# A stored order for five engines, replaced by another: packed attention followed by a gated MLP

## The chip, the cores and the metric

The kernel runs on 1 core of one Trainium2 chip. The metric is device time in microseconds (us) of one execution; lower is better. The kernel before takes 729.8 us (median of 3 runs, 729.75 to 729.95).

## What is computed

There are 8 batches of 8 heads, 576 positions, head size 64, and 32 "packed" queries per head. All inputs of the attention are float32. The MLP weights arrive as float64, eight bytes a value, and are reduced on the chip.

```
p_packed = softmax(p k^T / 8) v          # 32 packed rows per head
out      = softmax(q p_packed^T / 8) p_packed
x  = out, heads side by side             # 4608 tokens x 512
xn = x / rms(x) * rms_g
g  = xn w_gate ;  val = xn w_val         # 512 x 1536 each
y  = (silu(g) * val) w_out               # 1536 x 512
```

## The kernel before

The work is a set of some 270 chains. Each chain is a Python generator that yields a request (an engine and a modelled cost) before each small group of instructions that it emits. The names in `CHAINS` are these: `keys` loads p and k of a batch and transposes k; `stage1 b` computes the packed rows of batch b; `w 0` to `w 11` load one 1 MB float64 piece of w_gate or w_val, turn it into float32 in three passes (L585 on ACT; L588 to L592 on ACT, POOL or DVE; L599 on DVE) and, on each odd piece, find a scale per column group c (L647 to L672); `query u` and `attention u` treat unit u, which is 384 tokens; `pw b` multiplies the packed rows of batch b into the six column groups of the weights (matmuls L1299, after a scaling of a small tile at L1280 or L1282); `pw_evict b c` splits each product into two float16 halves (L548 on ACT, L550 on DVE); `mlp` runs unit after unit: twelve pairs of products of six matmuls (L1706), then three output tiles of 36 matmuls (L1733); `gated u f` evicts a pair (L1742, L1745) and splits it (L1757, L1760); `wo i` and `wo_split i` prepare w_out; `scales` makes the scales of unit 0; `store u i` evicts an output tile and stores it.

Which chain goes next is not decided by a rule at run time. The tuple `ORDER` (L43) has 2805 numbers, each the index of a chain in `CHAINS`. `Plan.run` (L301) walks through it and lets the named chain emit its next group. So `ORDER` fixes the order of the instructions within each of the five queues: PE, ACT, DVE, POOL, and SP, from which all loads and stores are issued. Each queue works in that order, and instructions of different queues are held together by semaphores only.

Two more things come from tables. `BY` (L346) says which engine does a step that several could do; there is one letter per instance (A for ACT, D for DVE, P for POOL), read by `way`. And `Plan.fill` (L279) puts filler matmuls (L1814, products of zeros that nobody reads) into the gaps which the plan's own clock expects on PE in the first stage; that clock uses the modelled costs and `FETCHES` (L58), a list of modelled delays of PE's instruction blocks. The `FETCHES` list reaches the program in no other way.

The first stage lasts until units 0 and 1 have their attention. Its chain for unit 0, by the lines that the rows name, is: scores (L1505, PE), row maxima and differences (L1526, DVE), exponentials (L1531, ACT), row sums and division (L1534 on, DVE), transposes (L1370, PE), copies of these (L1381 on ACT, L1384 on DVE), products with the packed rows (L1583, PE), sums of squares (L1602, ACT), the norm (L1619 on DVE, a power on POOL, L1635 on DVE), scaling (L1656 on ACT, a third of it on DVE), transposes (L1370), and the two float16 halves of the result (L1390 on ACT, L1392 on DVE). Then the first product of `mlp` can run.

Of the kernel before, what the change touches and what calls it, by code (L numbers as in the profile page):

```python
# [45 lines left out]
IN_TURN = range(18)  # L46

FILL = (0.5, 1.0, 400.0, 0.4, 2.5)

TABLE = 1.31  # L50

LOADING = (2.0, 385e3, 0.5)
TURNING = 2.2
COLD = 1.85
WINDOW, KEEP, HEAT = 3.4133, 0.39, 0.73
SWITCH = 0.093
FETCH = 4.3
FETCHES = (8.0, 8.0, 8.0, 8.0, 8.0, 8.0, 5.7397, 7.0078, 4.3, 4.3, 5.5211, 9.0647, 10.3428, 7.075, 6.652, 7.3144, 10.3813, 10.0522, 6.7016, 6.426, 4.3, 6.3087, 7.9214, 8.95, 4.8913, 7.311, 4.3, 4.3, 4.4226, 5.8673, 4.3, 4.3, 6.665, 7.2578, 5.85, 4.3, 7.0863, 14.3121, 6.5442, 9.189, 4.3, 4.3, 8.8812, 5.3336, 6.3223, 4.3, 4.3, 4.3, 6.1668, 7.5087, 4.8472, 4.3, 6.5501, 6.745, 4.3, 4.3, 4.3, 4.9924, 4.3, 4.3, 5.948, 4.3, 4.3)  # L58
FETCH_AT, FETCH_NEED, FETCH_SIZE = 128, 449, 256


def pe(n, count):

    return count * max(n / 2400 + 0.0025, 0.029)

ACT_COST = (0.093, 0.87e-3)
DVE_COST = (0.074, 0.953e-3)

# [13 lines left out]
def way(table, n, steps):  # L84
    by = BY[table][n]
    return by, steps[by]
# [15 lines left out]
class Plan:  # L102
# [160 lines left out]
    def fetched(self, t, cost, n):  # L263
# [4 lines left out]
        for k in range(max(0, (a - FETCH_NEED) // FETCH_SIZE), b // FETCH_SIZE + 1):  # L268
            for at in (FETCH_SIZE * k + FETCH_AT, FETCH_SIZE * (k - 1) + FETCH_NEED):
# [3 lines left out]
                if at == FETCH_SIZE * k + FETCH_AT:  # L273
                    self.avail[k] = x + (FETCHES[k] if k < len(FETCHES) else FETCH)
                else:
# [25 lines left out]
    def run(self, matmul):  # L301
        for n in ORDER:
            self.settle()
            chain = self.named[CHAINS[n]]
            assert isinstance(chain.ask, tuple) and chain.ask[0] in ENGINE, (chain.name, chain.key, chain.ask)
            e = ENGINE[chain.ask[0]]
            t = self.start(chain)
            kind, cost, *_ = chain.ask
            if e == "pe":
                self.fill(t, matmul)  # L310
                t = max(t, self.free["pe"])
            if kind == LOAD:
                self.free[e] = t + 0.45
                self.landed = max(self.landed, t + LOADING[0]) + cost / LOADING[1]
                seen = self.landed + LOADING[2]
            elif kind == TPOSE:
                issue = 0.1 + cost / 786432 * 3.5
                self.free[e] = t + issue
                self.landed = max(self.landed + 0.9 * issue, t + issue)
                seen = self.landed + TURNING  # L320
            else:
                if kind in (EXP, SILU) and kind != self.table:
                    self.table = kind
                if kind == DVE2 or (kind == POOL and len(chain.ask) < 4):
                    cost = self.port(kind, t, cost)
                if e == "pe":
                    cost = self.clocked(t, cost, 1.0 if len(chain.ask) < 4 else chain.ask[3])
                    cost = self.fetched(t, cost, 1 if len(chain.ask) < 5 else chain.ask[4])
                    self.tiled = kind == PET
                self.free[e] = t + cost  # L330
                seen = t + cost + LATENCY[kind]
            chain.end, chain.sent = seen, self.free[e]
            chain.since, chain.engine = 0.0, e
            self.go(chain)
        self.settle()
        assert not self.chains, [(c.key, c.ask) for c in self.chains]
# [6 lines left out]

LATER = {'attention': -1433.963, 'conv': 801.89, 'g': -1062.925, 'gated': 139.94, 'keys': 1179.512, 'mlp': 190.43, 'pw': -303.845, 'pw_evict': -510.85, 'query': 670.065, 'scales': -1237.656, 'stage1': 1107.652, 'store': -164.269, 'v': 1831.937, 'w': 752.946, 'wo': -103.455, 'wo_split': 661.626}

BY = {'low': 'PPAAPAAPAPAP', 'low_wo': 'PPPPPP', 'pgv': 'PPPAPDPPAAAPDAPAAP', 'norm_wo': 'DAAADA', 'keys': 'DADDADAAADAA', 'query': 'ADAAAA', 'hi0': 'DAADDAADDAAA', 'hi1': 'DDDAAAAAAAAA', 'hi_mixed': 'AAAAAAAAAAAA', 'hi_one': 'AAAAAAAAAAAA', 'lo0': 'DPPPDDDPDDPP', 'lo1': 'DPDDPDPDPDDD', 'lo_mixed': 'DPDPPDPDPDDD', 'lo_one': 'PDPDPPPPPDDD', 'gv': 'DPPPDP', 'wo_hi': 'AAPAAD', 'a1t': 'ADAAAA', 'a1t_late': 'AAAAAAAAAAAAAAAAAAAAAAAA', 'scaled': 'DAADDA', 'store': 'DDADDDDDDDDDDDDDDDDDDDDDDDDDDDDDDDDD'}  # L346

RAW_AT = (0, 1, 2, 3, 4, 5, 6, 7, 8, 4, 5, 6)
WO_AT = (8, 3, 7, 8, 3, 8)
# [1546 lines left out]
```

## Time and profile before

| | before |
|---|---|
| median of 3 runs | 729.8 us |
| the profiled execution | 729.18 us |
| its span, first to last instruction | 727.4 us |
| PE busy in the span | 708.4 us (97%) |
| DVE, ACT, POOL busy | 463.8, 454.9, 149.6 us |
| mean granted TensorE clock | 0.999 |

The table is read with one thing in mind: PE is busy for 97% of the span, but that counts the filler matmuls too, and all of its larger gaps lie in the first tenth of the span.

### The profile page before, as it was taken

To read this page: it belongs to the slowest core of one execution; us is meant where nothing else is said; L and a number is where in the kernel's file an instruction comes from. 1 tells how busy PE (TensorE), PEld (TensorE's weight loads), DVE (VectorE), ACT (ScalarE), POOL (GpSimd) and SP (SyncE) were. 2 spreads that over 40 slices of the span, in tenths; PEclk is the share of its full clock that TensorE was granted. 3 is DMA by queue.
4 is the path that set the end of the run, shared out by engine and by line. 5 is a ranking of instruction groups with operands and counts; after the bars stand their busy time and mean duration, and the time that the engine had idled before them with its cause. 6 is when DMAs were issued, how large, how long until landed. Compare 5 with 4: busy or idle time off the path is not lost. (4 is left out here: it accounts for less than half of the span.)

```text
span 727.4 us, 19349 instructions
## 1 busy us (share of the span) xinstructions
PE 708.4 (97%) x8099; PEld 424.9 (58%) x8099; DVE 463.8 (64%) x1053; ACT 454.9 (63%) x959; POOL 149.6 (21%) x168
## 2 busy tenths in 40 slices
PE   8789999999999999999999999999999999999997
PEld 5456655874564564784564564685554564784553
DVE  4689897778968858776758546666456443661320
ACT  3698986897786676675586575576375353570330
POOL 2158420102342343110120020010020030020210
PEclk9999999999999999999999999999999999999999
DMA  7997603767517534307625736613321414301001
GB/s 279 386 376 258 225 5 68 171 152 157 146 21 158 150 107 79 105 2 132 185 67 93 214 77 85 153 40 60 91 56 22 90 52 94 54 2 36 15 1 58
DMA packets 143239, 82.25 MB, mean 113 GB/s; under 512 B 105392, under 2 KB 128432, under 8 KB 143152
## 3 DMA queue, kind: packets, MB, share of 16 engines
q1 hardware_dynamic: 143152, 81.02, 43.3%
q8 instruction: 63, 1.03, 0.6%
q14 instruction: 24, 0.20, 0.1%
HBM read 47.97 MB, written 9.44 MB: 79 GB/s over the span
## 5 line engine op out<-in xcount | busy, mean ns | idle before, releaser
L1706 PEld LDWEIGHTS <-ring 128*128 128x128 f16 x2304 | 204.6, 98 | 85.3 <-issue 12.9
L1733 PEld LDWEIGHTS <-hall 128*128 128x128 f16 x1296 | 123.9, 98 | 147.8 <-issue 4.3
L1733 PE MATMUL pm_2x<-wo,hall 128*128 128x512 f16 x432 | 97.4, 379 | 0.0
L1760 POOL TENSOR_TENSOR hall<-t_0x,hall 128x384 f16<-128x384 f32 x39 | 36.0, 924 | 272.9 <-ACT hall L1757 252.0
L1733 PE MATMUL pm_3x<-wo,hall 128*128 128x512 f16 x360 | 80.9, 379 | 0.0
L1733 PE MATMUL pm_0x<-wo,hall 128*128 128x512 f16 x288 | 64.7, 379 | 0.2 <-DVE wo L767 0.2
L1760 POOL TENSOR_TENSOR hall<-t_1x,hall 128x384 f16<-128x384 f32 x35 | 33.1, 947 | 140.5 <-ACT hall L1757 131.1
L1757 ACT CAST hall<-t_1x 128x384 f16<-128x384 f32 x68 | 34.6, 509 | 22.7 <-DVE t_1x L1745 22.5
L1706 PE MATMUL pm_1x<-aTu_0x,ring 128*128 128x192 f16 (+1 forms) x348 | 48.1, 282 | 0.6 <-ACT t_0x L1742 0.6
L1733 PE MATMUL pm_1x<-wo,hall 128*128 128x512 f16 x216 | 47.8, 379 | 0.0
L1706 PE MATMUL pm_0x<-aTu_1x,ring 128*128 128x192 f16 (+1 forms) x330 | 44.7, 280 | 0.0
L1757 ACT CAST hall<-t_0x 128x384 f16<-128x384 f32 x68 | 34.7, 510 | 14.6 <-DVE t_0x L1745 14.4
L1706 PE MATMUL pm_2x<-aTu_1x,ring 128*128 128x384 f16 (+1 forms) x282 | 42.3, 292 | 0.0
L1706 PE MATMUL pm_0x<-aTu_0x,ring 128*128 128x384 f16 (+1 forms) x288 | 41.2, 286 | 0.1
L1706 PE MATMUL pm_3x<-aTu_0x,ring 128*128 128x384 f16 (+1 forms) x282 | 41.3, 289 | 0.0
L1531 ACT ACT_TABLE_LOAD x9 | 11.5, 1283 | 47.1 <-DVE e_0x L1528 47.1
L1706 PE MATMUL pm_1x<-aTu_1x,ring 128*128 128x384 f16 (+1 forms) x276 | 40.0, 288 | 0.0
L1706 PE MATMUL pm_3x<-aTu_1x,ring 128*128 128x192 f16 (+1 forms) x264 | 37.7, 286 | 0.0
L1706 PE MATMUL pm_2x<-aTu_0x,ring 128*128 128x384 f16 (+1 forms) x234 | 34.3, 289 | 0.9 <-issue 0.5
L1332 POOL TENSOR_TENSOR wgv<-o_0x,wgv 128x512 f16<-128x512 f32 x15 | 18.6, 1242 | 35.6 <-ACT wgv L1330 35.6
L1760 DVE TENSOR_TENSOR hall<-t_1x,hall 128x384 f16<-128x384 f32 x37 | 20.5, 554 | 7.5 <-ACT hall L1757 7.3
L1760 DVE TENSOR_TENSOR hall<-t_0x,hall 128x384 f16<-128x384 f32 x33 | 18.9, 571 | 6.2 <-ACT hall L1757 6.1
(910 smaller groups left out, 1353.8 us busy)
## 6 DMA issues: line engine op xcount, KB each, us to landing
out_dram<-o_0x SPq DMA_DIRECT2D x18, 256.0 KB, 2.2
out_dram<-o_1x SPq DMA_DIRECT2D x18, 256.0 KB, 2.4
hall<-in_moe_w_out_dram SPq DMA_DIRECT2D x4, 1024.0 KB, 6.7
wo<-in_moe_w_gate_dram SPq DMA_DIRECT2D x3, 1024.0 KB, 14.7
wo<-in_moe_w_val_dram SPq DMA_DIRECT2D x3, 1024.0 KB, 7.1
big_0x<-in_q_dram SPq DMA_DIRECT2D x3, 768.0 KB, 5.9
ring<-in_moe_w_gate_dram SPq DMA_DIRECT2D x2, 1024.0 KB, 11.8
ring<-in_moe_w_val_dram SPq DMA_DIRECT2D x2, 1024.0 KB, 12.8
```

The costliest lines, as they stand in the source:

```text
L1332: nc.gpsimd.tensor_tensor(wgv16[:, c, k, 1], st, wgv16[:, c, k, 0], ALU.subtract)
L1531: nc.scalar.activation(e, e, AF.Exp, scale=esc)
L1706: nc.tensor.matmul(psi[:, :, o : o + n], pw[:, g, lw, w, f * P : (f + 1) * P], aT[:, :, la, g, o : o + n], start=(j == 0), stop=(j == 5),)
L1733: nc.tensor.matmul(po, hall[:, ft, lh, ts], wo[:, ft, 1 - lw, :], start=(n == 0), stop=(n == 3 * NFT - 1))
L1757: (nc.scalar.copy if by == "A" else nc.vector.tensor_copy)(hall[:, ft, 0, :], t)
L1760: (nc.gpsimd if by == "P" else nc.vector).tensor_tensor(hall[:, ft, 1, :], t, hall[:, ft, 0, :], ALU.subtract)
```

## The change

`ORDER` is replaced by another tuple of the same 2805 entries: every chain occurs just as often. 27 letters in eleven of the `BY` tables change. `FETCHES` gets other values for 33 of its 63 entries. No function is changed, and neither is any buffer.

```diff
-ORDER = (0, 0, 0, 3, 0, 0, 0, 0, 0, 0, 0, 0, 0, 0, 0, 0, 0, 0, 16, 16, 0, 0, 0, 34, 3, 3, ...
+ORDER = (0, 0, 0, 3, 0, 0, 0, 0, 0, 0, 0, 0, 0, 0, 3, 16, 16, 1, 4, 1, 0, 0, 0, 0, 0, 0, ...
-FETCHES = (8.0, 8.0, 8.0, 8.0, 8.0, 8.0, 5.7397, 7.0078, 4.3, 4.3, 5.5211, 9.0647, ...
+FETCHES = (8.0, 8.0, 8.0, 8.0, 8.0, 8.0, 7.8005, 6.644, 4.3, 4.3, 6.3583, 9.2726, ...
 BY = {...
-  'low': 'PPAAPAAPAPAP', 'pgv': 'PPPAPDPPAAAPDAPAAP', 'norm_wo': 'DAAADA',
+  'low': 'APDAPAAPAPAP', 'pgv': 'DADPPDPPPAAPDAPAAP', 'norm_wo': 'DADDDA',
-  'keys': 'DADDADAAADAA', 'query': 'ADAAAA', 'hi1': 'DDDAAAAAAAAA', 'lo1': 'DPDDPDPDPDDD',
+  'keys': 'DDAAADAAADAA', 'query': 'ADDAAA', 'hi1': 'ADAAADAAAAAA', 'lo1': 'DDPDDPPDPDDD',
-  'gv': 'DPPPDP', 'a1t': 'ADAAAA', 'scaled': 'DAADDA', 'store': 'DDADDD...'
+  'gv': 'PPPPPP', 'a1t': 'AAAAAA', 'scaled': 'DAAAAD', 'store': 'DAADDD...'
```

What that does to each queue follows from counting the entries. Of PE's 899 groups 121 stand at another place, and nearly all of these are swaps of neighbours. On SP, ACT and DVE about half of the groups stand at another place, over the whole program, mostly by a few places. In the first stage the moves that matter for the steps below are:

```
SP    the first piece of unit 1's query, 192 KB:  before w 3      -> after w 5
      unit 1's second query piece:                after w 9       -> before w 9
      v 0, first half:                            after w 0       -> before w 0
ACT   first pass of w 1 (L585):                   after the squares of batch 0 -> before them
      first pass of w 7:                          before the first pw_evict    -> after its first half
      first and second pass of w 10:              before pw_evict 0 2          -> after it
      first pass of w 9 and of w 11, copies of keys and query: places swapped with neighbours;
      a keys copy now stands before L1390 of unit 0
DVE   last pass of w 6 and one pw_evict split:    after L1384 of unit 0 -> before it
      first batch's pg (L1230):                   after the scale of w 1 -> before L1526
      scaling of pw 0 0 and pw 0 2:               POOL -> DVE
ACT   scaling of pw 0 1: POOL -> ACT;   POOL  scaling of pw 0 3: ACT -> POOL
POOL  three scale products (L670 to L672) of column groups 0 and 4: DVE -> POOL
PE    the matmuls of pw 0 0 now stand before the scale of w 3
```

## Rows read from the trace of the kernel before

**Rows 1.** Busy time of each engine by stretch: us and instructions, clock, DMA share, GB/s.
```profile
0.00:60.00 60.00, 49.20 (x782) 32.42 (x783) 41.04 (x94) 40.84 (x70) 22.94 (x37) 1.00 0.97 352
60.00:115.00 55.00, 52.97 (x716) 31.84 (x714) 49.15 (x113) 48.50 (x95) 24.78 (x27) 1.00 0.38 125
115.00:700.00 585.00, 582.93 (x6499) 350.29 (x6498) 370.39 (x845) 364.52 (x793) 101.92 (x105) 1.00 0.41 91
700.00:727.40 27.40, 23.25 (x108) 10.36 (x106) 3.25 (x6) 1.04 (x3) 0.00 (x0) 0.98 0.11 39
```
**Rows 2.** The same view for the filler line L1814 alone (PE, PEld).
```profile
0.00:62.00 62.00, 16.22 (x56) 5.56 (x56) 1.00 0.95 344
```
**Rows 3.** The same view, all engines, over the loading of the weights.
```profile
20.00:60.00 40.00, 32.01 (x495) 21.40 (x487) 33.54 (x73) 33.59 (x58) 17.85 (x18) 1.00 1.04 383
```
**Rows 4.** Waits of PE: total us, times, longest.
```profile
PE psb L1370 <- DVE tiny_10x L531: 1.6, 1, 1.6
...
PE psb L1631 <- ACT a_0x L969: 0.8, 1, 0.8
```
**Rows 5.** Timeline of PE: start us, us, line, tiles; idle before in brackets.
```profile
42.37 0.32 PE L1583 MATMUL psa<-pk_0x,aT_0x 32*128 32x64 f32 x2
...
53.67 0.89 PE L1370 MATMUL psa<-ident,e_0x 128*128 128x128 f32 x6
...
58.92 1.14 PE L1706 MATMUL pm_1x<-aTu_0x,ring 128*128 128x384 f16 x6
```
**Rows 6.** Timeline of SP's queue: the query piece that is moved.
```profile
11.39 3.17 SPq L1417 DMA_DIRECT2D big_5x<-in_q_dram  x1
```
**Rows 7.** Timeline of ACT along unit 0's attention chain.
```profile
21.23 1.13 ACT L585 ACTIVATE wgv<-ring 128x1024 f32<-128x1024 f32 x1 [0.19 <-DMA ring<-in_moe_w_val_dram]
22.27 0.24 ACT L1178 COPY misc<-pm_0x 64x128 f32<-64x128 f32 x1
...
31.40 0.92 ACT L1531 ACTIVATE e_0x<-e_0x,qk 128x768 f32<-128x768 f32 x1
...
35.80 1.17 ACT L585 ACTIVATE wgv<-wo 128x1024 f32<-128x1024 f32 x1 [0.57 <-DMA wo<-in_moe_w_gate_dram]
...
37.92 0.63 ACT L1381 ACTIVATE aT_0x<-psb 128x512 f32<-128x512 f32 x1
...
53.09 0.98 ACT L1656 ACTIVATE e_0x<-e_0x,trio_3x 128x256 f32<-128x256 f32 x2
...
55.89 0.90 ACT L1390 ACTIVATE aTu_0x<-psa 128x768 f16<-128x768 f32 x1
56.59 0.68 ACT L881 COPY big_4x<-pm_1x 128x512 f32<-128x512 f32 x1
```
**Rows 8.** Timeline of DVE along the same chain.
```profile
27.28 0.95 DVE L1526 TENSOR_REDUCE t_0x<-psa 128x24 f32<-128x768 f32 x1
...
41.12 0.41 DVE L1384 TENSOR_SCALAR aT_0x<-psb 128x256 f32<-128x256 f32 x1
...
43.05 1.22 DVE L599 SCALAR_TENSOR_TENSOR wgv<-wgv,wo 128x1024 uint32<-128x1024 uint32 x1
44.18 0.69 DVE L550 SCALAR_TENSOR_TENSOR ring<-pm_1x,ring 128x512 f16<-128x512 f32 x1
...
50.22 0.69 DVE L550 SCALAR_TENSOR_TENSOR ring<-pm_3x,ring 128x512 f16<-128x512 f32 x1 [0.52 <-ACT ring L548]
...
51.76 0.15 DVE L1635 TENSOR_REDUCE tiny_18x<-psb 128x1 f32<-128x3 f32 x1
...
57.59 0.95 DVE L1392 SCALAR_TENSOR_TENSOR aTu_0x<-psa,aTu_0x 128x768 f16<-128x768 f32 x1
```
**Rows 9.** Line L1282 by engine and tile: duration ns min/median/max, first and last start.
```profile
L1282 POOL TENSOR_TENSOR pgh_0x<-pg_0x,gv_r x3: 615/1525/1690, 35.7 to 53.4; 128x256 f32<-128x256 f32 x3
...
L1282 DVE TENSOR_TENSOR pgh_1x<-pg_0x,gv_r x1: 411/411/411, 64.9 to 64.9; 128x256 f32<-128x256 f32 x1
```
**Rows 10.** Timeline of POOL: the second of the three scale products of group 1.
```profile
46.41 2.31 POOL L671 TENSOR_SCALAR gv_sc<-gv_r,gmax_r 128x1 f32<-128x1 f32 x1
```

More of the change, by code (lines that the diff above doesn't have):

```diff
@@ L57 @@
 FETCH = 4.3
-FETCHES = (8.0, 8.0, 8.0, 8.0, 8.0, 8.0, 5.7397, 7.0078, 4.3, 4.3, 5.5211, 9.0647, 10.3428, 7.075, 6.652, 7.3144, 10.3813, 10.0522, 6.7016, 6.426, 4.3, 6.3087, 7.9214, 8.95, 4.8913, 7.311, 4.3, 4.3, 4.4226, 5.8673, 4.3, 4.3, 6.665, 7.2578, 5.85, 4.3, 7.0863, 14.3121, 6.5442, 9.189, 4.3, 4.3, 8.8812, 5.3336, 6.3223, 4.3, 4.3, 4.3, 6.1668, 7.5087, 4.8472, 4.3, 6.5501, 6.745, 4.3, 4.3, 4.3, 4.9924, 4.3, 4.3, 5.948, 4.3, 4.3)
+FETCHES = (8.0, 8.0, 8.0, 8.0, 8.0, 8.0, 7.8005, 6.644, 4.3, 4.3, 6.3583, 9.2726, 9.106, 7.079, 6.652, 8.0216, 10.2325, 10.6118, 6.1454, 6.6127, 4.3, 4.4692, 9.5888, 10.3636, 5.1421, 7.6155, 4.3, 4.7555, 4.4226, 5.6093, 4.3, 4.3, 5.4002, 7.2428, 5.9726, 4.3, 6.8864, 13.4124, 6.652, 8.1551, 4.3, 4.3, 9.6067, 6.2304, 6.1229, 4.3, 4.3, 4.3, 6.8771, 7.2375, 4.5566, 4.3, 7.0853, 5.7308, 4.3, 4.3, 4.3, 5.2882, 4.3, 4.3, 6.2882, 4.3, 4.3)
 FETCH_AT, FETCH_NEED, FETCH_SIZE = 128, 449, 256
@@ L344 @@
 LATER = {'attention': -1433.963, 'conv': 801.89, 'g': -1062.925, 'gated': 139.94, 'keys': 1179.512, 'mlp': 190.43, 'pw': -303.845, 'pw_evict': -510.85, 'query': 670.065, 'scales': -1237.656, 'stage1': 1107.652, 'store': -164.269, 'v': 1831.937, 'w': 752.946, 'wo': -103.455, 'wo_split': 661.626}
-BY = {'low': 'PPAAPAAPAPAP', 'low_wo': 'PPPPPP', 'pgv': 'PPPAPDPPAAAPDAPAAP', 'norm_wo': 'DAAADA', 'keys': 'DADDADAAADAA', 'query': 'ADAAAA', 'hi0': 'DAADDAADDAAA', 'hi1': 'DDDAAAAAAAAA', 'hi_mixed': 'AAAAAAAAAAAA', 'hi_one': 'AAAAAAAAAAAA', 'lo0': 'DPPPDDDPDDPP', 'lo1': 'DPDDPDPDPDDD', 'lo_mixed': 'DPDPPDPDPDDD', 'lo_one': 'PDPDPPPPPDDD', 'gv': 'DPPPDP', 'wo_hi': 'AAPAAD', 'a1t': 'ADAAAA', 'a1t_late': 'AAAAAAAAAAAAAAAAAAAAAAAA', 'scaled': 'DAADDA', 'store': 'DDADDDDDDDDDDDDDDDDDDDDDDDDDDDDDDDDD'}
+BY = {'low': 'APDAPAAPAPAP', 'low_wo': 'PPPPPP', 'pgv': 'DADPPDPPPAAPDAPAAP', 'norm_wo': 'DADDDA', 'keys': 'DDAAADAAADAA', 'query': 'ADDAAA', 'hi0': 'DAADDAADDAAA', 'hi1': 'ADAAADAAAAAA', 'hi_mixed': 'AAAAAAAAAAAA', 'hi_one': 'AAAAAAAAAAAA', 'lo0': 'DPPPDDDPDDPP', 'lo1': 'DDPDDPPDPDDD', 'lo_mixed': 'DPDPPDPDPDDD', 'lo_one': 'PDPDPPPPPDDD', 'gv': 'PPPPPP', 'wo_hi': 'AAPAAD', 'a1t': 'AAAAAA', 'a1t_late': 'AAAAAAAAAAAAAAAAAAAAAAAA', 'scaled': 'DAAAAD', 'store': 'DAADDDDDDDDDDDDDDDDDDDDDDDDDDDDDDDDD'}
 RAW_AT = (0, 1, 2, 3, 4, 5, 6, 7, 8, 4, 5, 6)
```

2 lines of the change are left out of this document (1 added, 1 removed).

## The prediction

> **What bounds the kernel now.** I read the table by stretch first [rows 1]. PE's idle time is the stretch minus PE's busy time: 10.80 us up to 60 us, 2.03 from 60 to 115, 2.07 over the 585 us to 700, and 4.15 at the end, 19.05 in all. The last stretch is the tail: after PE's last matmul one tile is evicted and stored, and the last 12 entries of the order are the same in both tuples. From 60 us on PE is the bound: its work does not change, so the kernel ends earlier only by what PE idles less, or fills less with useless matmuls. The filler line has 56 matmuls, 16.22 us of busy time, all before 62 us [rows 2]. So what a new order can win lies before the first product of unit 0, which starts at 58.92 us [rows 5].
>
> What holds that product back? Between 20 and 60 us the loads run at 383 GB/s with a DMA share of 1.04, that is full, while DVE and ACT are busy for 33.5 and 33.6 of 40 us and PE works for 32.0, fillers among it [rows 3]. No engine is full there; the chain of unit 0's attention is what PE waits for, and it is in turn late at each place where its step stands in a queue behind a conversion of weights. The list of waits says the same: the longest wait of PE in the span is the 1.6 us before the transposes L1370 [rows 4], and the longest after 115 us is 0.8.
>
> I then followed that chain through the timelines of ACT and DVE [rows 7, 8]. The reader is to see in each row which instruction stands just before it in its queue: L1531 at 31.40 us follows a conversion pass that waited for its load; L1381 at 37.92 follows two passes of w 6, the first of which waited 0.57 us for its load; L1384 at 41.12, L1635 at 51.76, L1656 at 53.09, L1390 at 55.89 and L1392 at 57.59 each stand behind conversions or evictions of pw.
>
> **The change, step by step.** Each step is placed by the new order in the queue and by the durations of the rows.
>
> 1. *The query piece.* 192 KB, at 383 GB/s [rows 3, 6] 0.51 us of the stream, goes behind w 5. So w 3, w 4 and w 5 land 0.51 us earlier; from w 6 on the same bytes stand ahead as before. L1531, which is held by w 4's pass, moves from 31.40 to 30.89. Bounds: 0 if the queue's own pace of issue decides (its piece took 3.17 us to issue), 0.51 if bytes do. I take 0.5.
>
> 2. *The first pass of w 1 before the squares.* It waits for its load till 21.23 us [rows 7], so the copy L1178, which stood right behind it at 22.27, now has the squares of batch 0 between, and comes later by four short instructions (an estimate: at most 0.24 us each, the time of the copy itself, so up to 1.0 us). The scores follow it. But DVE comes to L1526 at 27.28 only [rows 8], after three last passes at 1.22 us; the new order uses the wait for the copy for one of them. The slack between 22.27 and 27.28 holds the scores and those passes. I take 0; without that cover it would be 1.0.
>
> 3. *The first pw group.* Its scaling leaves POOL, where three instances took 615 to 1690 ns, for DVE, where one took 411 [rows 9]; its matmuls and the first half of its eviction come 1 to 2 us earlier. This is not on the chain of unit 0: the first product waits for L1390 and L1392, 18 us after. I take 0.
>
> 4. *L1381.* It stays behind the passes of w 6, whose load has the same bytes ahead of it. So it stays at 37.92, and the 0.5 us of step 1 is lost here. This is the step that makes the sum small.
>
> 5. *L1384.* The last pass of w 6 (1.22 us, row at 43.05) and a split of pw (0.69) are put ahead of it [rows 8], while one scale product group leaves DVE and DVE is 0.5 us ahead. Upper bound: 41.12 + 1.22 + 0.69 = 43.03. I take 42.0. The cover: PE reaches L1583 at 42.37 [rows 5] only after the matmuls of pw 0 1, in both orders. So 0; with 43.03 plus the 0.41 of the copy it would be 43.44 - 42.37 = 1.07 us late.
>
> 6. *From L1602 to L1635.* The squares on ACT stay where they are. On DVE the 1.9 us of step 5 are already done, 0.41 for pw 0 2 is added, and the 0.52 us that DVE idled before the row at 50.22 goes, since pw_evict 0 2 now stands ahead of the passes of w 10 on ACT. L1635 comes between 0 and 1.9 us earlier than 51.76; I take 0.9, nearest to the two smaller terms together (0.41 + 0.52).
>
> 7. *L1656 and L1390.* The passes of w 10, the same work as before, now stand between the eviction and L1656: of the 0.9 I keep 0.3 (between -0.5 and 0.9). Then the keys copy that came behind L1390 at 56.59 [rows 7] comes ahead of it, at a pitch of about 0.5 (0.68 busy). L1390: 55.89 - 0.3 + 0.5 = 56.1.
>
> 8. *L1392.* At 57.59 it follows the last pass of w 11, which follows POOL's pass, which follows the scaling of pw 0 4, which follows L1635. Earlier by up to 0.9; but L1390 must be done: 56.1 + 0.9 = 57.0. So 0.5 to 0.6 earlier, and the first product of unit 0 at about 58.4 instead of 58.92.
>
> PE's own swaps of neighbours move work past the first product and back, at no cost while PE is full. The rest of the program, over which about half of ACT's and DVE's groups stand elsewhere by a few places, has 2.03 + 2.07 us of idle PE to lose and no bound from the rows on what it might gain; I take 0, and plus or minus 1.
>
> Sum: -0.5 us. The profiled execution took 729.18 us, 727.4 of it the span; this gives 728.7 for it. The median of the runs lies 0.62 above that execution, so the predicted median is 729.8 - 0.5 = 729.3.
>
> At one place the Trainium skill speaks against the change, beside a row here: L671 on POOL took 2.31 us for a 128x1 operand [rows 10] and L1282 there between 615 and 1690 ns for one shape [rows 9]. The page "SBUF — State Buffer", section "Who interferes with whom", says that VectorE and GpSimd share a port pair as an exclusive lock, and that a VectorE instruction with two SBUF inputs holds off a GpSimd one that reads SBUF. By this the scale products that go to POOL, and the scaling of pw 0 3 ahead of the power of unit 0's norm, would each wait for a DVE pass; the spread in the rows agrees.
>
> **The rivals.**
>
> *POOL becomes late (no change).* Scaling pw 0 3 on POOL stands just ahead of the power of unit 0's norm. If it takes 1690 instead of 615 ns [rows 9], the power comes 1.1 us later, which eats the 0.9 of step 6: L1635's followers, w 11 and L1392 stay where they were. Sum 0: 729.8. For it: the slow instances in rows 9 and 10 lie in this stretch. Against it: POOL is busy for 17.9 of 40 us [rows 3] and loses more work than it gets.
>
> *The whole chain moves (faster).* If step 4's loss doesn't happen (w 6 lands earlier too, so that L1381 moves by 0.5) and the keys copy is hidden, then 0.5 + 0.9 reach the first product, 57.5, and one of the 2.03 us of idle PE after 60 us goes with it: -2.4, 727.4. For it: 10.80 us of idle PE and 16.22 of fillers are there to be had. Against it: each step behind a load is only as early as the load.
>
> *Unit 0's chain is put behind other work (slower).* Place: L1384 behind the pass of w 6 and the split, L1390 behind the keys copy. Price: 1.07 (step 5's upper end) + 0.68 = 1.75 us, 731.5. It decides from the point at which L1384 ends after 42.37, when PE stands at L1583 with nothing else ahead. For it: both moves are in the order. Against it: DVE's earlier start in step 5.
>
> That the change does nothing at all to PE's idle time is within the first rival.
>
> **How the numbers follow.** A measurement of this kernel can tell from no change what exceeds about 0.2%, 1.46 us. Forecast (-0.5, from -1.4 to +0.5): 0.42. POOL late (0): 0.15. Faster (727.4): 0.25. Slower (731.5): 0.18. Of the forecast a little lies beyond 1.46, and of the two outer cases a little lies within, so faster 0.25, same 0.58, slower 0.17. The forecast's own range is 728.4 to 730.3; to hold 8 in 10 the range reaches to 727.5 below, near the faster case, and to 731.2 above, short of the slower one.
>
> **What would show it.** Right: L1531 near 30.9 and L1381 still near 37.9; L1583 within 0.3 us of 42.4; L1635 near 50.9; the first L1706 near 58.4; PE's idle time up to 60 us near 10.3 with about as many fillers; the other stretches as they were. Wrong: L1583 after 43, or the first L1706 outside 57.8 to 59.2, or an idle time of PE after 115 us that differs by over a microsecond, which would mean that the moves in the rest of the program count.

## The result and the profile after

| | us |
|---|---|
| before, median of 6 runs | 729.88 |
| after, median of 6 runs | 734.18 (733.42 to 735.98) |
| ratio | 1.0064, 95% interval 1.0050 to 1.0078 |
| after, profiled execution | 733.85, span 732.1 |
| predicted | 729.3, range 727.5 to 731.2 |

The change makes the kernel 4.3 us slower. This lies above the predicted range and above the price of the slower rival, 731.5.

The table by stretch of the kernel after, with the columns of [rows 1]: stretch, its length, busy time of PE, PE's loads, DVE, ACT and POOL, granted clock, DMA share, GB/s.

```profile
0.00:60.00 60.00, 50.53 (x781) 33.40 (x782) 42.12 (x91) 41.20 (x72) 21.85 (x37) 0.97 0.98 351
60.00:115.00 55.00, 50.52 (x700) 30.13 (x698) 48.17 (x102) 45.97 (x87) 25.89 (x30) 1.00 0.37 123
115.00:700.00 585.00, 582.33 (x6488) 349.31 (x6486) 371.44 (x848) 363.23 (x793) 104.56 (x106) 1.00 0.41 91
700.00:732.10 32.10, 27.96 (x137) 13.13 (x135) 5.42 (x9) 3.96 (x8) 0.92 (x1) 0.97 0.09 33
```

PE's idle time is 9.47 up to 60 us (10.80 before), 4.48 from 60 to 115 (2.03), 2.67 to 700 (2.07) and 4.14 at the end (4.15); there are 55 fillers, 16.34 us of them (56 and 16.22 before). The 9.47 looks like the smaller idle time that was forecast for the head, but it shows little: in the traces of the runs below this number lies between 10.3 and 12.1 with the old order up to the first product, and between 9.4 and 11.4 with the new one. The growth from 60 to 115 us stands where the prediction took 0, plus or minus 1. The idle time grew by 1.7 in all and the span by 4.7: the other 3.0 stand as busy time of PE. The clock of 0.97 in the first stretch may be a part of that: from 23.9 to 27.3 us the granted clock is 0.5, 1.2 GHz instead of 2.4, after three microseconds in which PE was busy for 0.74, 0.10 and 0.56. But the run on pair 9 below has such a fall too, and PE is busy for 709.5 us in it, 1.1 more than before and not 3.0. I can't place the rest; the ends of matmuls are modelled, so the starts of the same matmuls, below, are the better account.

The waits of PE in the kernel after (total, times, longest), where [rows 4] had 1.6 before L1370 and 0.8 before L1631:

```profile
PE pm_2x L659 <- DVE tiny_13x L657: 2.1, 1, 2.1
PE psb L1370 <- DVE tiny_10x L531: 1.4, 1, 1.4
...
PE pm_0x L1193 <- ACT junk_0x L1160: 1.2, 1, 1.2
PE pm_2x L1706 <- ACT pts_0x L1183: 1.2, 1, 1.2
PE psb L1631 <- ACT a_0x L969: 1.0, 1, 1.0
PE pm_3x L1706 <- DVE ring L550: 1.0, 1, 1.0
```

The same wait before L659 in the kernel before:

```profile
PE pm_2x L659 <- DVE tiny_13x L657: 1.0, 1, 1.0
```

The reader is to see four that the list of before did not have at this length: 2.1 us before L659 (at 42.21), 1.2 before L1193 (at 23.3), and two before the products L1706: 1.0 for the eviction L550 (at 73.3) and 1.2 for the copy L1183 (at 93.6). The last two stand on PE's path behind the first product.

The chain that the prediction followed, in the kernel after, on ACT, DVE and PE in turn (before: [rows 5, 7, 8]):

```profile
31.10 0.95 ACT L1531 ACTIVATE e_0x<-e_0x,qk 128x768 f32<-128x768 f32 x1
...
38.12 0.59 ACT L1381 ACTIVATE aT_0x<-psb 128x512 f32<-128x512 f32 x1
...
56.54 0.89 ACT L1390 ACTIVATE aTu_0x<-psa 128x768 f16<-128x768 f32 x1
```
```profile
39.84 1.99 DVE L599 SCALAR_TENSOR_TENSOR wgv<-wgv,wo 128x1024 uint32<-128x1024 uint32 x1
41.75 0.41 DVE L657 TENSOR_REDUCE tiny_13x<-pm_2x 128x2 f32<-128x256 f32 x1
42.08 0.68 DVE L550 SCALAR_TENSOR_TENSOR ring<-pm_1x,ring 128x512 f16<-128x512 f32 x1
42.68 0.41 DVE L1384 TENSOR_SCALAR aT_0x<-psb 128x256 f32<-128x256 f32 x1
...
51.91 0.15 DVE L1635 TENSOR_REDUCE tiny_19x<-psb 128x1 f32<-128x3 f32 x1
...
57.68 0.94 DVE L1392 SCALAR_TENSOR_TENSOR aTu_0x<-psa,aTu_0x 128x768 f16<-128x768 f32 x1
```
```profile
43.33 0.32 PE L1583 MATMUL psa<-pk_0x,aT_0x 32*128 32x64 f32 x2
...
55.09 0.82 PE L1370 MATMUL psa<-ident,e_0x 128*128 128x128 f32 x6
...
58.50 1.15 PE L1706 MATMUL pm_2x<-aTu_0x,ring 128*128 128x384 f16 x6
...
59.71 0.63 PE L877 MATMUL pm_0x<-ident,big_0x 128*128 128x128 f32 x4
```

The first product comes at 58.50, forecast 58.4. But L1583 is 0.96 later than before and L1370 1.42 later, and four transposes L877 at 59.71 now stand behind the product, which stood ahead of it. From here I followed the lag, that is how much later each matmul starts than the same one in the kernel before: -0.42 at the first product, +1.69 at 78 us, +2.99 at the first matmul L1733 (98.14 instead of 95.15), +3.71 at unit 1's first product, +4.4 to 4.7 from 250 us on.

### The profile page after: what moved, and what is told of

It reads as the page before. It is cut to its first block, busy times and chain, and to the rows that moved or that the text cites. A ratio compares the mean times of both kernels' runs of the same rounds, so it can differ in the third digit from the quotient of the medians.

```text
span 732.1 us, 19344 instructions
## 1 busy us (share of the span) xinstructions
PE 711.4 (97%) x8099; PEld 426.0 (58%) x8099; DVE 467.2 (64%) x1048; ACT 454.4 (62%) x957; POOL 153.2 (21%) x172
## 4 chain that ended last, share of the span: by engine, by line
PE 49%; DVE 1%; DMA 1%; ACT 1%; issue 0%; ACTq 0%; DVEq 0%
PE pm_2x L1733 7%; PE pm_0x L1733 7%; PE pm_2x L1706 6%; PE pm_1x L1706 6%; PE pm_3x L1706 5%; PE pm_3x L1733 5%; PE pm_0x L1706 4%; PE pm_1x L1733 2%; PE pm_1x L1311 1%; PE psa L1512 1%; DMA aT_0x<-hl_0x 1%; PE psa L1592 0%; PE pm_3x L1311 0%; PE pm_0x L1311 0%; PE psb L1142 0%; PE pm_2x L1311 0%
## 5 line engine op out<-in xcount | busy, mean ns | idle before, releaser
L1706 PEld LDWEIGHTS <-ring 128*128 128x128 f16 x2304 | 204.6, 98 | 87.7 <-issue 15.9
L1733 PEld LDWEIGHTS <-hall 128*128 128x128 f16 x1296 | 123.9, 98 | 147.8 <-issue 4.3
L1733 PE MATMUL pm_0x<-wo,hall 128*128 128x512 f16 x468 | 105.2, 379 | 0.4 <-DVE wo L767 0.2
L1760 POOL TENSOR_TENSOR hall<-t_0x,hall 128x384 f16<-128x384 f32 x38 | 36.0, 947 | 227.9 <-ACT hall L1757 217.9
L1760 POOL TENSOR_TENSOR hall<-t_1x,hall 128x384 f16<-128x384 f32 x36 | 35.2, 977 | 201.8 <-ACT hall L1757 191.2
L1733 PE MATMUL pm_3x<-wo,hall 128*128 128x512 f16 x288 | 64.5, 379 | 0.0
L1733 PE MATMUL pm_2x<-wo,hall 128*128 128x512 f16 x288 | 64.4, 379 | 0.0
L1733 PE MATMUL pm_1x<-wo,hall 128*128 128x512 f16 x252 | 56.7, 379 | 0.0
L1706 PE MATMUL pm_2x<-aTu_0x,ring 128*128 128x192 f16 (+1 forms) x348 | 49.2, 285 | 1.6 <-ACT pts_0x L1183 1.2
L1706 PE MATMUL pm_1x<-aTu_1x,ring 128*128 128x384 f16 (+1 forms) x300 | 43.5, 288 | 0.1
L1706 PE MATMUL pm_2x<-aTu_1x,ring 128*128 128x192 f16 (+1 forms) x324 | 43.6, 279 | 0.0
L1706 PE MATMUL pm_1x<-aTu_0x,ring 128*128 128x192 f16 (+1 forms) x312 | 42.4, 280 | 0.0
L1706 PE MATMUL pm_3x<-aTu_1x,ring 128*128 128x192 f16 (+1 forms) x288 | 41.2, 286 | 0.0
L1706 PE MATMUL pm_0x<-aTu_0x,ring 128*128 128x192 f16 (+1 forms) x276 | 38.0, 281 | 0.6 <-ACT t_0x L1742 0.3
L1706 PE MATMUL pm_0x<-aTu_1x,ring 128*128 128x384 f16 (+1 forms) x240 | 36.6, 294 | 0.0
L1706 PE MATMUL pm_3x<-aTu_0x,ring 128*128 128x384 f16 (+1 forms) x216 | 35.4, 304 | 1.0 <-DVE ring L550 1.0
L1332 POOL TENSOR_TENSOR wgv<-o_1x,wgv 128x512 f16<-128x512 f32 x15 | 18.6, 1242 | 35.0 <-ACT wgv L1330 35.0
L1760 DVE TENSOR_TENSOR hall<-t_0x,hall 128x384 f16<-128x384 f32 x36 | 21.0, 583 | 5.2 <-ACT hall L1757 5.1
L550 DVE SCALAR_TENSOR_TENSOR ring<-pm_1x,ring 128x512 f16<-128x512 f32 x27 | 18.5, 685 | 8.1 <-ACT ring L548 8.1
```

The costliest lines, as they stand in the source:

```text
L550: nc.vector.scalar_tensor_tensor(lo, x, s, hi, ALU.mult, ALU.subtract)
L1332: nc.gpsimd.tensor_tensor(wgv16[:, c, k, 1], st, wgv16[:, c, k, 0], ALU.subtract)
L1706: nc.tensor.matmul(psi[:, :, o : o + n], pw[:, g, lw, w, f * P : (f + 1) * P], aT[:, :, la, g, o : o + n], start=(j == 0), stop=(j == 5),)
L1733: nc.tensor.matmul(po, hall[:, ft, lh, ts], wo[:, ft, 1 - lw, :], start=(n == 0), stop=(n == 3 * NFT - 1))
L1760: (nc.gpsimd if by == "P" else nc.vector).tensor_tensor(hall[:, ft, 1, :], t, hall[:, ft, 0, :], ALU.subtract)
```

## The experiments

In the edits, OLD and NEW are the orders of the kernels before and after, each with its own choice of engines; "mlp 0" is the step of the first product, and the head is all that stands ahead of it. A hybrid does every step that NEW has ahead of the cut and then, in OLD's order, all that is left (or the other way round), so that both parts do the same work as before. Each time is a median beside runs of the kernel before on the same chip, 729.7 to 729.8; intervals are those of the ratio.

| run | median us | ratio, 95% |
|---|---|---|
| NEW to mlp 0, then OLD | 733.41 | 1.0026 to 1.0056 |
| OLD to mlp 0, then NEW | 734.26 | 1.0051 to 1.0075 |
| OLD to mlp 12 (78 us), then NEW | 732.5 | 1.0024 to 1.0051 |
| OLD to mlp 24 (95 us), then NEW | 731.45 | 1.0013 to 1.0031 |
| OLD to mlp 60 (125 us), then NEW | 731.2 | 1.0012 to 1.0030 |
| OLD to mlp 0, then NEW, three moves undone | 731.8 | 1.0019 to 1.0042 |

**Which side of the first product?** Two hybrids.

```diff
-ORDER = NEW
+ORDER = NEW[until mlp 0] + OLD[what is left]     # first run
+ORDER = OLD[until mlp 0] + NEW[what is left]     # second run
```

> The new order (with its engines) up to the first product of unit 0, then the old order for everything that is left. Theory A, the loss has two sources of about equal weight: the head delivers the first product on time (58.5) but with about 1.3 us of PE work pushed behind it (PE's busy time up to 60 us rose by 1.33 with a stretch at half clock, 1.2 GHz, from 23.8 to 27.2), and the new order after it adds its own stalls (1.16 before the products at 93.6, 0.97 at 73.3, and about 1.7 after 98 us): the old order behind it takes the second source away, about 731.5. Rival B, the head makes everything later by itself, so that the old order behind it stalls as well: 734. Rival C, the loss lies wholly behind the first product: 729.4 to 729.9.

> The mirror image: the old order (with its engines and its fillers) up to the first product, then the new order. Theory A: only the stalls of the later part are left, 729.9 + 2.5 to 3.0 = 732.4 to 732.9, with the wait before the products that stand behind the copy L1183 still over 1 us. Rival B: 729.9, no loss, since all of it comes from the head. Rival C: 734.

The second gave 734.26 (733.90 to 735.03, the clock at 0.999 or 1.0 in each run). The old head with the new rest is as slow as the whole change: theory A, which gave the head 1.3 to 1.7 us of it, is wrong, and so is B; C holds in this run. Its waits between 58 and 125 us are those of the kernel after:

```profile
PE pm_1x L1706 <- ACT pts_0x L1183: 1.2, 1, 1.2
PE pm_2x L1706 <- DVE ring L550: 1.0, 1, 1.0
...
PE psb L1631 <- DVE ru_1x L1623: 0.5, 1, 0.5
```

The first gave 733.41, but in two groups: 730.58 and 730.93 with a mean granted clock of 0.999, 733.25 to 734.16 in the four runs at 0.992 to 0.995. So the new head costs about 1.0 at full clock, and 3.5 to 4.4 in the runs of the lower clock; C, which had it at 729.4 to 729.9, is wrong here, and B's 734 is met only by these runs. In the table by stretch of its profiled execution (at 0.992) the fall is seen behind PE's thinnest stretch of that time:

```profile
40.00:42.00 2.00, 0.37 (x2) 0.09 (x1) 2.00 (x2) 1.94 (x5) 1.03 (x1) 1.00 1.04 388
42.00:44.00 2.00, 1.52 (x48) 0.89 (x48) 2.00 (x5) 2.00 (x3) 0.00 (x0) 1.00 1.06 381
44.00:46.00 2.00, 2.00 (x46) 1.88 (x43) 1.93 (x6) 0.93 (x3) 1.06 (x1) 0.56 1.05 380
...
50.00:52.00 2.00, 2.00 (x44) 1.10 (x30) 1.19 (x4) 2.00 (x10) 0.57 (x1) 0.73 0.98 294
```

PE is busy for 0.37 of 2 us while it waits 2.1 before L659, and from 44.2 to 51.1 it runs at 1.2 GHz. That the wait makes the clock fall is not shown: the traces of the kernel after and of the run with the squares first have the same wait of 2.1, and no fall behind it.

**Pair 9, and the squares.** Two small edits of the kernel after.

```diff
 PE:  products mlp 18
-     L1168 (batch 1), mlp 19, mlp 20
+     mlp 19, mlp 20, L1168 (batch 1)
-ACT: L1178, L1183, L767 (wo 1), L1742 (pair 9)
+ACT: L1742 (pair 9), L767 (wo 1), L1178, L1183
```

> The changed kernel with sixteen neighbouring steps near 91 to 94 us put back into the old order among themselves: PE does both products of pair 9 before the transposes L1168 of batch 1, and ACT does their SILU (L1742) and the second wo conversion ahead of the copies L1178 and L1183, no longer behind them. Theory A: PE's wait of 1.16 us before the products (on the copy L1183) goes, the lag of the later stages falls from 3.7 to about 2.5, 733.0. Rival: the copy L1178 on DVE is still late behind two passes of 1.28 us, and the wait only passes to the next step that needs it: 734.2, with a wait of a microsecond elsewhere between 90 and 100 us.

The place itself, in the kernel after on ACT:

```profile
91.14 0.24 ACT L1178 COPY misc<-pm_2x 64x128 f32<-64x128 f32 x1
93.25 0.27 ACT L1183 COPY pts_0x<-pm_2x 128x128 f32<-128x128 f32 x1 [1.87 <-DVE misc L1178]
93.41 1.05 ACT L767 COPY wo<-o_0x 128x1024 f16<-128x1024 f16 x1
94.36 0.59 ACT L1742 ACTIVATE t_1x<-pm_3x,usc_0x 128x384 f32<-128x384 f32 x1
```

The copy in the kernel before:

```profile
91.55 0.27 ACT L1183 COPY pts_0x<-pm_3x 128x128 f32<-128x128 f32 x1 [0.45 <-DVE misc L1178]
```

In the kernel after, ACT idles 1.87 ahead of the copy L1183 for DVE, whose half of L1178 stands behind two passes of 1.28, and the SILU of pair 9 is behind both copies in ACT's queue. With the edit that wait is gone from the list, and the first L1733 comes at 97.1 instead of 98.1; the profiled run took 733.0. The median does not show it: 735.34 (1.0069 to 1.0095), four of five runs at a clock of 0.993 to 0.995 and 735.1 to 737.1. By its time the run decides nothing.

```diff
-ACT: L585 (w 1), then the squares L1160
+ACT: the squares L1160, then L585 (w 1)
```

> The changed kernel with one step moved: the first pass of w 1 on ACT stands behind the squares of batch 0 again, as in the old order (with its POOL companion). Theory A: PE's wait of 1.2 us before the transposes L1193 at 23.3 goes, and with it the stretch at 1.2 GHz that follows; PE's busy time up to 60 us falls by about 1.3, and that backlog is missing behind the first product: 732.9. Rival: the head is held by DVE (L1384 at 42.7 behind its two passes), so that scores that come earlier only wait longer: 734.2, with the granted clock of the head at 1.0 all the same.

736.12 (1.0067 to 1.0091). The wait before L1193 and the fall at 24 us are gone from the profile, but the two runs at 0.999 took 734.12 and 734.31, the kernel after's time, and three at 0.995 took 736.1 to 736.6. Theory A is wrong here too: this fall costs nothing that the runs can tell. The runs at 0.995 must have others, but of those executions there is no trace.

**Moving the cut.** With the old head every run has a clock of 0.999 or 1.0, so the rest can be measured stretch by stretch.

```diff
+ORDER = OLD[until mlp 12] + NEW[what is left]    # then mlp 24, mlp 60
```

> The old order up to unit 0's twelve first products (about 78 to 83 us), then the new order. Theory D, formed after the old head with the new rest came out at 734.3 without any fall of the clock: the loss sits behind the first product, in separate places, and each goes when its stretch gets the old order. By the lag of that run's products: 1.7 us between 59 and 78, 1.3 between 78 and 95, 0.7 between 98 and 114, about 1.1 later. So here 734.3 - 1.7 = 732.6. Rival E: PE is held by what comes after (the loads and the chain of unit 1), so that time won in one place is only waited out in the next: 734.3.

> The old order up to unit 0's 24th product (about 95 us), then the new order. Theory D: 734.3 - 1.7 - 1.3 = 731.3, with neither the wait on the ring's eviction L550 (0.97) nor the one on the copy L1183 (1.2). Rival E: over 733.

> The old order up to the first product of unit 1 (about 125 us), then the new order. Theory D: 734.3 - 1.7 - 1.3 - 0.7 = 730.6, that is about 0.8 to 1.1 over the kernel before, and the rest of it in small waits between 140 and 400 us. Rival F, the order behind 125 us is as good as the old one: 729.8.

732.5, 731.45 and 731.2: theory D holds and E falls. From one cut to the next the order costs 1.8 (59 to 78 us), 1.0 (to 95), 0.2 (to 125, less than the runs can tell) and 1.5 behind 125 us (0.9 to 2.2), so F falls as well. The traces split the last two otherwise: 0.6 up to 125 us, and behind it 1.1 in pieces of 0.2 to 0.4, at about 144, 158, 190, 204 and 243 us. Which moves make them was not tried. In the two runs with the later cuts the lag also grows by 0.5 near 72 us, where the order is still the old one and PE waits 0.3 for L550; the trace of the kernel before has no such wait, so half a microsecond between two traces need not come from the order.

**One instruction of POOL.** The old head with the new rest, and one move.

```diff
 POOL:
+ L590 hall<-hall (wo 0)
  L670, L671, L672 (scale products of w 7)
- L590 hall<-hall (wo 0)
```

> The old head with the new rest, and in it one instruction moved: POOL does wo 0's pass (L590, 1.10 us) ahead of the three scale products of w 7 (L670 to L672, 58.42 to 59.45) again, as in the old order; all other engines keep their order. Theory D, that this is what starts the loss between 59 and 78: DVE's wait of 0.99 us before L599 at 60.67 goes, what is queued behind it (the keys copy L881, both steps of gated 0 0, which free the buffer that ACT waits 1.70 us for) comes about 1 us earlier, and so do the two evictions of pw 0 5; PE's wait of 0.97 us on the second of DVE's parts goes: 733.3. Rival G: the evictions are late by their own place on ACT, behind two casts and with a pass of 1.15 us between their halves, whatever DVE does: 734.3, with the wait of about a microsecond at 73.5 still there.

The place without the move, from the old head with the new rest, on POOL, DVE, ACT and PE in turn (start, us, line; idle before in brackets):

```profile
58.42 0.27 POOL L670 TENSOR_SCALAR gv_sc<-tiny_16x,gmax 128x1 f32<-128x1 f32 x1
...
59.53 1.10 POOL L590 TENSOR_SCALAR hall<-hall 128x1024 uint32<-128x1024 uint8 x1
...
68.20 1.13 POOL L590 TENSOR_SCALAR hall<-hall 128x1024 uint32<-128x1024 uint8 x1
70.90 0.91 POOL L1760 TENSOR_TENSOR hall<-t_1x,hall 128x384 f16<-128x384 f32 x1 [1.57 <-ACT hall L1757]
```
```profile
60.67 1.22 DVE L599 SCALAR_TENSOR_TENSOR wo<-wo,hall 128x1024 uint32<-128x1024 uint32 x1 [0.99 <-POOL hall L590]
...
68.38 1.34 DVE L1760 TENSOR_TENSOR hall<-t_0x,hall 128x384 f16<-128x384 f32 x1
...
70.99 1.91 DVE L599 SCALAR_TENSOR_TENSOR wo<-wo,hall 128x1024 uint32<-128x1024 uint32 x1
72.82 0.68 DVE L550 SCALAR_TENSOR_TENSOR ring<-pm_2x,ring 128x512 f16<-128x512 f32 x1
```
```profile
69.84 0.58 ACT L1742 ACTIVATE t_0x<-pm_1x,usc_0x 128x384 f32<-128x384 f32 x1 [1.70 <-DVE hall L1760]
...
71.00 0.58 ACT L548 ACTIVATE ring<-pm_2x 128x512 f16<-128x512 f32 x1
```
```profile
73.55 1.14 PE L1706 MATMUL pm_2x<-aTu_0x,ring 128*128 128x384 f16 x6 [0.97 <-DVE ring L550]
```

It is read from the bottom: PE waits 0.97 for L550, which waits for DVE's pass (1.91 beside POOL's L1760 at 70.90, where the same pass took 1.22 before) and for ACT's L548 at 71.00; that stands behind the SILU at 69.84, which waited 1.70 for the buffer that DVE's L1760 frees; and L1760 took 1.34 beside POOL's pass at 68.20, which had started first. In the kernel before, DVE had started first, and it was POOL's pass that grew:

```profile
67.70 1.47 POOL L590 TENSOR_SCALAR hall<-hall 128x1024 uint32<-128x1024 uint8 x1
```
```profile
67.58 0.56 DVE L1760 TENSOR_TENSOR hall<-t_0x,hall 128x384 f16<-128x384 f32 x1
...
69.40 1.22 DVE L599 SCALAR_TENSOR_TENSOR wo<-wo,hall 128x1024 uint32<-128x1024 uint32 x1
```

With the move DVE's wait of 0.99 is gone, and the time is 733.67 (1.0043 to 1.0068), 0.6 less, at the edge of what five runs tell; in the traces the products from 78 us on start 0.46 earlier. But L1760 still takes 1.34, and PE's wait stays:

```profile
PE pm_2x L1706 <- DVE ring L550: 1.0, 1, 1.0
```

So rival G is right on the wait, and D on half of the gain.

```diff
 ACT:
+ L548 (pw 0 5, first half)
  L1742 (pair 2)
+ L548 (pw 0 5, second half)
  L1757, L709
- L548
  L1757, L585 (wo 4)
- L548
 DVE:
  L1745 (pair 2)
+ L550, L550 (pw 0 5)
  L599 (wo 3)
- L550
  L961, L962
- L550
```

> The old head with the new rest, and in it the eviction of pw 0 5 moved: on ACT its first half (L548) stands ahead of the SILU (L1742) that waits 1.70 us for its buffer, and the second half right behind that SILU, ahead of two casts, a norm and a pass of wo 4; on DVE both halves (L550) stand ahead of the pass L599 that took 1.91 us. Theory G, from the run with the POOL swap, where the wait of 0.97 us on L550 stayed: these two moves are what that wait is made of; it goes, and the program gains 1.0: 734.3 - 1.0 = 733.3. Rival H: the place is bound by the buffer of gated 0 0 (the SILUs of the pairs that follow), and the products only wait for pm instead of the ring: 734.3.

733.53 (1.0044 to 1.0069), 0.7 less, and the wait on L550 is gone: G holds. A wait of 0.7 of the matmuls L1043 for ACT's L969, which the run without the move does not have, takes a part of the gain back.

**All three together.**

> The old head with the new rest, with three moves undone together: wo 0's pass on POOL ahead of the scale products of w 7; the eviction of pw 0 5 early on ACT and DVE; the sixteen steps about pair 9 (products and SILU ahead of the transposes and copies of batch 1). Theory D: the gains add up, 0.6 + 0.7 (single runs of the first two) + 1.2 (the wait on the copy L1183): 734.3 - 2.5 = 731.8, close to the old order up to 95 us (731.45). Rival L: they overlap, or give way to other waits of the new order: 733.0 or more.

731.8, to the tenth. The sixteen steps about pair 9, the four of the eviction and the one of POOL, of 2805, are 2.5 of the 4.5 us by which the new rest is slower.

**The head.** The query piece alone, in the kernel before:

```diff
 SP:
- L1417 big_5x<-in_q_dram
  L626 (w 3), ..., L626 (w 5)
+ L1417 big_5x<-in_q_dram
```

> The kernel before with step 1 alone: the query piece of 192 KB goes behind the loads of w 5 instead of ahead of w 3. As predicted: L1531 at 30.9 instead of 31.4, L1381 stays at 37.9, first product unchanged, 729.8. Rival: the 0.5 us carries through to the first product, 729.3. Or the scores' query arrives too late and PE waits for it before L877 or L1438: 730.3.

729.78, ratio 1.0002 (0.9993 to 1.0011): no change, as the prediction's steps 1 and 4 had it. On ACT:

```profile
31.22 0.93 ACT L1531 ACTIVATE e_0x<-e_0x,qk 128x768 f32<-128x768 f32 x1
...
38.22 0.57 ACT L1381 ACTIVATE aT_0x<-psb 128x512 f32<-128x512 f32 x1
```

L1531 gained 0.2 of the 0.5, and L1381 did not move forward.

Then the head in two halves, `NEW[until L1531] + OLD` and `OLD[until L1531] + NEW[until mlp 0] + OLD`:

> The new order up to the exponential L1531 of unit 0 (31 us; with it the first pass of w 1 ahead of the squares), then the old order. It asks which part of the new head makes the clock fall in most runs (the new head with the old rest: 730.6 and 730.9 in two runs at a granted clock of 0.999, 733.3 to 734.2 in four at 0.992 to 0.995; the old head: never under 0.999). Theory J, the thin stretch from 21 to 24 us (PE busy for 0.74, 0.10 and 0.56 of three us) does it: falls here too, some runs at 0.997 or less and 1 to 3 us longer, the others about 730. Rival K: the falls come from 40 to 44 us, behind the wait of 2.1 us before L659: none here, all runs within 729.5 to 730.5.

> The old order up to the exponential L1531, the new one from there to the first product of unit 0, then the old one again. Theory J: no fall of the clock, since PE's stretch from 21 to 24 us is as before; what is left is the later L1384 (two passes of DVE ahead of it) with PE's wait of about 2 us before L659: 0.5 to 1.0 over the kernel before, 730.5. Rival K: falls here, runs of 733.

729.95 (0.9994 to 1.0012) and 730.69 (1.0005 to 1.0022). The first half costs nothing that the runs can tell: three of its runs have a clock of 0.996 to 0.998, and they took 729.6 to 730.0. So J is wrong in its price. The second half costs 1.0 without a fall of the clock in any run, as J has it, and K is wrong for the halves alone. Its trace shows where: L1583 starts at 42.11, earlier than before, and the first product is only 0.26 late, but by 73 us the products lag by 1.3, behind these waits (0.6 before in the first, none in the second):

```profile
PE pm_2x L1706 <- ACT t_0x L1742: 1.0, 1, 1.0
...
PE pm_1x L1706 <- DVE ring L550: 0.3, 1, 0.3
```

No run takes these waits away one by one. The falls that cost something came only with both halves: in the second half alone the pass L599 of w 6 on DVE came at 39.40 and took 1.22, in the whole new head with the old rest, a little later, it came at 40.11, behind POOL's L590, and took 1.99:

```profile
40.11 1.99 DVE L599 SCALAR_TENSOR_TENSOR wgv<-wgv,wo 128x1024 uint32<-128x1024 uint32 x1
```
```profile
39.91 1.13 POOL L590 TENSOR_SCALAR hall<-hall 128x1024 uint32<-128x1024 uint8 x1
```

The next run exchanges it with its neighbour on DVE.

```diff
 DVE:
- L550 (pw 0 0, first half)
  L599 (w 6)
+ L550 (pw 0 0, first half)
```

> The new head with the old rest (733.4; 730.6 to 730.9 in the runs at a clock of 0.999), and in the head two neighbours on DVE exchanged: the last pass of w 6 (L599, at 40.11 and 1.99 us long there) comes ahead of the first split of pw 0 0 (L550, for which DVE was idle 0.63). Theory M: L599 took 1.99 instead of 1.22 since it started 0.2 behind POOL's pass L590 (39.91, 1.13 long) and the two run one after the other; put first it takes 1.22, the wait of 2.1 before L659 falls to about 0.5, PE is not thin there any more, and with it the falls at 44 us go: all runs within 729.8 to 730.9. Rival N: the long pass is a matter of its data, 1.9 to 2.0 us wherever it stands, and the falls stay: 733.

730.94 (1.0009 to 1.0027): ten of eleven runs lie between 730.5 and 731.3; one at 0.994 took 732.87. Before the swap four of six lay above 733. On DVE and on POOL with the swap:

```profile
39.16 1.26 DVE L599 SCALAR_TENSOR_TENSOR wgv<-wgv,wo 128x1024 uint32<-128x1024 uint32 x1 [0.32 <-ACT aT_0x L1381]
```
```profile
39.45 1.18 POOL L672 TENSOR_SCALAR wo_sc<-tiny_12x,gsq 128x1 f32<-128x1 f32 x1
40.72 1.12 POOL L590 TENSOR_SCALAR hall<-hall 128x1024 uint32<-128x1024 uint8 x1
```

The pass takes 1.26 now, not 1.99, and the one that waits is POOL: its L672, 0.34 without the swap, takes 1.18. PE's wait before L659 falls from 2.1 to 1.3 (0.5 was expected). Theory M holds for the pass and for nearly all of the falls that cost time; three more runs have a clock of 0.996 to 0.998 and took 730.8 to 731.1. A cost of 1.1 stays.

Last, the kernel before with L657 ahead of L550 on DVE:

```diff
 DVE:
- L550 (pw 0 0, first half)
  L657
+ L550 (pw 0 0, first half)
```

> The kernel before with two neighbours on DVE exchanged: the maximum L657 at 40.78 comes ahead of the split L550 at 40.18, for which DVE had waited 1.01 us. PE's wait of 1.02 before L659 at 41.25 falls to under 0.3. If the chain of unit 0 bounds the head as my prediction had it, L1583 comes up to 0.7 earlier and the kernel ends at 729.1 to 729.4. Rival: L1583 waits for L1384 all the same, or the gain is given back before the first product by the next conversions: 729.7.

730.21 (0.9995 to 1.0013). The wait before L659 went from 1.0 to 0.5 and L1583 came 0.35 earlier, but the first product did not. The rival holds: half a microsecond in the head was not worth anything by itself here. Of all versions tried none is faster than the kernel before.

## Why the prediction was wrong

The step that failed is the last term of the sum: "The rest of the program ... has 2.03 + 2.07 us of idle PE to lose and no bound from the rows on what it might gain; I take 0, and plus or minus 1." It measured +4.5 (old head, new rest: 734.26). Its traces show it as the products' wait of 1.0 for the eviction at 73 us, that of 1.2 for the copy at 94 us, one of 0.5 before L1631 near 115 us, and small pieces behind 125 us. I had read the small idle time behind 60 us as a property of the work, PE is full there. It is a property of the order: between two products each SILU, cast and eviction has to free its buffer within the time of a product or two, and the old order did that. What a new one can lose there is not bounded by the idle time that is left. My test for this term looked behind 115 us only, where the idle time grew by 0.6; the 2.45 us of new idle time from 60 to 115 would have passed it. Of the other signs of being wrong one came, L1583 after 43; the first L1706 lay inside its bounds.

By the steps:

1. The query piece: right in kind, 0.2 to 0.3 instead of 0.5 (31.10, alone 31.22).
2. w 1's pass ahead of the squares: 0 in the time, as taken (new order to 31 us: 729.95), though it brought a wait of 1.2 that I did not foresee. In the trace of the kernel after the clock falls behind that wait; in the trace of the new order to 31 us it does not, with the same wait and as thin a stretch of PE.
3. Not tested by itself; it lies in the half that costs 1.0.
4. L1381 at 38.12: right.
5. L1384 at 42.68, not 42.0. I had both ends and took the middle; a pass beside POOL's took 1.99 instead of 1.22, and the upper end was the nearer one. L1583 was 0.96 late, and the price I gave without cover was 1.07. But it was not L1384 that held it: L1384 was done at 43.09, and PE came to L1583 from the matmuls of pw 0 1 at 43.33. These were the cover, and they were late themselves, behind L659, which waited 2.1 for L657; and L657 stands behind the same pass on DVE. Where the pass took 1.22 (the new order from 31 us on), L1384 came at 41.49 and L1583 at 42.11.
6. L1635 at 51.91 instead of 50.9, 0.15 later than before. The sum of this step was wrong: it counted the scaling of pw 0 2, 0.41 more work on DVE, as a gain. DVE's idle time of 0.52 did go, but L1621 took 0.63 beside POOL's scaling of pw 0 3 (0.23 before), and step 5 had left DVE no lead: it came to L657 at 45.96, before at 45.98.
7. L1390 at 56.54, forecast 56.1; the keys copy ahead of it was counted, step 6's loss was not.
8. L1392 at 57.68, forecast 57.0; the first product at 58.50, forecast 58.4, yet by luck, because PE put four transposes behind it. In the kernel before, that product had not waited for L1392 (done at 58.54) at all, but stood behind these transposes, without idle time, until 58.92. A right time for one instruction said nothing on the work that was done by then.

The head as a whole: I gave -0.5; it costs about +1.0 with the old rest at full clock, and 2.3 to 3.6 more in runs of a lower mean clock (in the one with a trace a fall lies between 44 and 51 us). In the kernel after, the 1.0 is not seen beside the 4.5: its runs at a clock of 0.997 and 0.999 took 733.4 to 734.5, no more than the old head with the new rest. In both traces the products wait at 73 us for the eviction, and behind it they lag by 1.7 and 1.9. Its two runs at 0.992 and 0.994 took 735.8 and 736.0.

The rivals: the slower one had a place (L1384, L1583) that does come late, and a price (1.75) not far from what the head costs; but the kernel is as slow without it, and the second half of the head costs its 1.0 with L1583 on time. The first, a late POOL, had the right pair of engines and the wrong victim: I let POOL wait for DVE and priced it in one place, where DVE's own passes on the path grew, 0.7 us at a time. The Trainium skill's page "SBUF — State Buffer", section "Who interferes with whom", says that it is the order of issue that decides who of the two blocks. The swap above agrees: 1.99 and 0.34 became 1.26 and 1.18. The trace of the second half alone does not, by the starts in the profile: POOL's L672 started at 39.26, 0.14 ahead of the pass, and still it was POOL that took longer (1.40; the pass 1.22). Spans on POOL are rough, so which of the two was issued first there stays open. What I had weighed of that rule was half of it.

Open stays which moves behind 125 us make the last 1.5, and what lets the clock fall at 44 us: with a wait of 2.1 before L659 four of six runs of one kernel have a lower clock and lose time, with 1.3 one of eleven, but two traces with 2.1 have no fall there.

## What to carry to other kernels

Where an order was tuned, the stretch in which the bounding engine hardly waits is where a new order can lose most, as here: count what must be freed between two of its instructions, and in whose queue that stands, before such a stretch is put down as 0. A cut that takes one order up to a step and the other behind it does the same work and tells the stretches apart; here the first two cuts came out within 0.2 us of what the lag in one trace had said, and three moves undone together gave the sum that two runs and one wait had promised. Two engines that block each other turned shifts of a few tenths of a microsecond into 0.7 to 0.8 us on DVE, so the durations of the old trace held only where the two kept their places.

## What the runs showed of the hardware

A granted clock of 0.5 for 3.4 us at 24 us cost nothing that the runs can tell: the traced execution of the kernel after, with that fall, took 733.85, and the one with the squares first, without it, 734.12. The runs of the new order to 31 us at 0.996 to 0.998 took 729.6 to 730.0, though there is no trace that shows where their clock fell. In contrast the execution with another one for 6.8 us from 44 to 51 us was over 3 us longer than those at 0.999: there PE was busy for all of the time at half speed. The same kernel had both kinds of run on one chip (730.6 and 734.2), so a median of a few runs can hide an effect of a microsecond, as in the run on pair 9. And a DVE instruction of two SBUF inputs that started 0.2 us behind one of POOL took 1.99 instead of 1.22 us, an L1760 1.34 instead of 0.56; where DVE was ahead, POOL's took 1.18 instead of 0.34 and 1.47 instead of 1.13.
